# Turning token rows for an expert layer: four TensorE transposes per 128 slots and two copies across partitions

## The chip, the cores and the metric

The kernel runs on one core of one Trainium2 chip. The metric is device time in microseconds for one execution of the whole program. Before the change the median of three runs is 1355.3 us (1355.29 to 1356.96). The profiled execution, from which all other times here are taken, spans 1351.2 us at a granted TensorE clock of 0.995.

## What is computed

Eight sequences of 3584 tokens with 192 channels first pass a causal convolution over 7 tokens, with one softmax-normalised set of taps for each of 8 heads of 24 channels. Then each token goes through one of 8 experts, a two-layer perceptron with 1024 hidden units. The expert is the argmax of the token's own logits, unless a local gate tells the token to keep the expert of the token before it. All numbers are fp32.

```python
x = conv(x, softmax(weight))                       # (8, 3584, 192)
logits = x @ w_gate; local_gate = sigmoid(x @ w_local)
for b in range(B):
    prev_e = -1
    for s in range(S):
        fresh_e = argmax(logits[b, s])
        e = fresh_e if s == 0 or local_gate[b, s] < 0.5 else prev_e   # (or fresh_e if there is none)
        prev_e = e
        p = softmax(logits[b, s])
        h = maximum(x[b, s] @ w1[e], 0.0)          # 192 -> 1024
        out[b, s] = p[e] * (h @ w2[e])             # 1024 -> 192
```

## The kernel before

The 28672 tokens are cut into 16 groups of 1792. For each group the kernel convolves (for most groups ScalarE does the first tap of each head and VectorE the other six), computes the logits, decides the expert of every token, and writes each token's row of 259 words to a place in DRAM that belongs to its expert (`slots`). A row holds the gate factor, the token's number, 192 channels from column `Y0` on, and then 64 channels again, before the token's number once more. The rows go out by indirect DMAs that GpSimd issues (`put`, L777), 128 rows each.

The expert layer reads those rows back in blocks: a single block has 128 slots of one expert (n = 1), a double block has 256 (n = 2). There are 55 singles and 87 doubles in a normal run: singles first, since few rows are ready then, doubles through the middle, and singles at the end for the rests. Two spare blocks at the very end run only if the data need them.

For each block i the order on TensorE is written out by hand:

1. `hidden(i)` (L960): w1 times the turned rows `xT`. The contraction over 192 channels is cut in three steps d of 64. The two 64-row halves of the array work side by side: the upper half makes hidden units 0 to 511 and the lower half 512 to 1023, and each needs all 192 channels, so each holds its own three pieces of 64 channels, with the weights laid out on the host to match. The hidden units come in two lots (`two`), each followed by two relus on ScalarE into `hT` (L965).
2. `turn(i + 1)` (L360 for the transposes, L946 for the copy): the rows `xg` of the next block are turned into `xps` (PSUM), and ScalarE copies them into `xT` (SBUF, one buffer).
3. `output(i)` (L977): w2 times `hT`, for k = 0 and 1 and eight pieces m of the hidden units. The pieces 0, 1, 4, 5 are made by the first pair of relus and come first, the pieces 2, 3, 6, 7 by the second pair. ScalarE (L985) and VectorE (L989) scale and add the two halves' results, and GpSimd scatters them to `out` (L993).

In between, `step(...)` issues convolution and routing work for later groups to ScalarE (L378) and VectorE (L388), and `put(relu)` issues a scatter of rows that waits for the relus. With n = 2 and many rows left to scatter, one more `put` waits for the copy out of `xps` (`copied`). Rows and weights are loaded three blocks ahead, and the load of weights waits until the output matmuls of an earlier block let go of their buffer.

A transpose turns 64 slots (one half of the partitions) by 128 channels. In `turn`, step d takes the 128 channels from 64 d on:

```python
for d in range(KD):                                # 3
    for k in range(n):
        src = xg[:, k, Y0 + d * DR:Y0 + (d + 2) * DR]
        for half in range(2):
            turn_half(at[:, half, d, k, :], src, half)
```

With d = 0 the upper 64 partitions get channels 0 to 63 and the lower ones 64 to 127; with d = 1 they get 64 to 127 and 128 to 191; with d = 2, 128 to 191 and, through the repeated 64 channels of the row, 0 to 63. That makes six transposes per 128 slots, in pairs over the two halves of the slots.

Of the kernel before, what the change touches and what calls it, by code (L numbers as in the profile page):

```python
# [17 lines left out]
P = 128  # L18
B, S, D = 8, 3584, 192
# [11 lines left out]
TB = PT // NB  # L31
# [3 lines left out]
DR = P // 2  # L35
KD = D // DR
FK = F // P
BT = 2 * UT
KT = BT // P
# [22 lines left out]
Y0 = 2  # L62
IX = DG - 1
# [18 lines left out]
def kernel(  # L82
# [10 lines left out]
    nc = tc.nc  # L93
# [44 lines left out]
    with tc.tile_pool(name="scr", bufs=1) as scr:  # L138
        w = scr.tile([1, H, KC], F32, name="w")
# [50 lines left out]
    def z_tile():  # L190
        return yt.tile([P, 3 * NH * TB + NB * DR], F32, name="z")
# [3 lines left out]
    def wide(g, xv, y_sb, both):  # L195

        lps = yps_p.tile([P, 512], F32, name="yps")[:, :4 * TB].rearrange("p (q s) -> p q s", s=TB)  # L200
        count = [0]

        def mine():
            count[0] += 1
            return both and count[0] % 2 == 0

        def convolve(half, heads):
            bs = slice(half * NH, (half + 1) * NH)
            for h in heads:
                ps = hps_p.tile([P, 512], F32, name="hps")[:TB, :NH * GS]  # L210
                nc.tensor.matmul(ps, lhsT=hank[:NI, h, :],
                                 rhs=xv[:NI, bs, h * GS:(h + 1) * GS], start=True, stop=True)
                to = y_sb[:TB, bs, Y0 + h * GS:Y0 + (h + 1) * GS]
                at = ps.rearrange("p (b d) -> p b d", d=GS)
                if mine():
                    nc.vector.tensor_scalar(to, at, rz[:TB, h:h + 1], None, Alu.mult)
                else:
                    nc.scalar.activation(to, at, Act.Copy, scale=rz[:TB, h:h + 1])
                yield

        def again(half):
            bs = slice(half * NH, (half + 1) * NH)
            nc.gpsimd.tensor_copy(yr[:, bs, :], y_sb[:TB, bs, Y0 + P:Y0 + D])
            nc.gpsimd.tensor_copy(y_sb[:TB, bs, Y0 + D:IX], y_sb[:TB, bs, Y0:Y0 + DR])

        def turned(half, qs):
            at = half * 3 * NH // 2
            for q in qs:
                tps = hps_p.tile([P, 512], F32, name="hps")[:, :4 * TB].rearrange(
                    "p (u s) -> p u s", s=TB)  # L230
                for u in range(4):
                    b = half * NH + (q * 4 + u if q < 2 else 2 * u)
                    src = (y_sb[:TB, b, Y0:Y0 + P] if q < 2
                           else yr[:, b:b + 2, :].rearrange("p b d -> p (b d)"))
                    nc.tensor.transpose(tps[:, u, :], src, identity=ident[:TB, :TB])
                leave = nc.vector.tensor_copy if mine() else nc.scalar.copy
                leave(yT[:, at + 4 * q:at + 4 * q + 4, :], tps)
                yield

        def products():  # L240
            for j in range(4):
                u = j // 2 * 3 * NH // 2 + j % 2 * 4
                nc.tensor.matmul(lps[Q * j:Q * j + Q], lhsT=wgb[:, 0, :], rhs=yT[:, u:u + 4, :],
                                 start=True, stop=False, skip_group_check=True)
            for i in range(2):
                for j in range(4):
                    u = j // 2 * 3 * NH // 2 + NH + j % 2 * 2
                    nc.tensor.matmul(lps[Q * j:Q * j + Q, i::2, :], lhsT=wgb[:, 1 + i, :],
                                     rhs=yT[:, u:u + 2, :], start=False, stop=(i == 1),
                                     skip_group_check=True)  # L250

        yield from convolve(0, range(H))
        zy = z_tile()
        yT = zy[:, :3 * NH * TB].rearrange("p (u s) -> p u s", s=TB)
        yr = zy[:TB, 3 * NH * TB:].rearrange("p (b d) -> p b d", d=DR)
        again(0)
        yield from convolve(1, range(5))
        yield from turned(0, (0, 1))
        yield from convolve(1, range(5, H))
        yield from turned(0, (2,))  # L260
        again(1)
        yield from turned(1, range(3))
        products()
        if both:
            nc.vector.tensor_copy(lsb[:, :2, :], lps[:, :2, :])
            nc.scalar.copy(lsb[:, 2:, :], lps[:, 2:, :])
        else:
            nc.scalar.copy(lsb, lps)
        yield
        ltp = yps_p.tile([P, 512], F32, name="yps")[:TB].rearrange("p (q c) -> p q c", c=P)  # L270
        for q in range(4):
            nc.tensor.transpose(ltp[:, q, :], lsb[:, q, :], identity=ident)
        lt = sm.tile([P, NB, E + 1], F32, name="lt")[:TB]
        mark["lt", g] = nc.vector.tensor_copy(lt.rearrange("p (j q) e -> p j q e", q=4),
                              ltp.rearrange("p q (j c) -> p j q c", c=Q)[:, :, :, :E + 1])
        got[g] = lt
# [34 lines left out]
    rows = cst.tile([Q, 2, Q], F32, name="rows")  # L311
# [247 lines left out]
    def gathered(ps):  # L559
        xg = xp.tile([P, KT, DG], F32, name="xg")  # L560
        nc.scalar.copy(xg[:, 0, :Y0 + D], ps[:, :Y0 + D])
        nc.scalar.copy(xg[:, 0, Y0 + D:IX], ps[:, Y0:Y0 + DR])
        nc.scalar.copy(xg.bitcast(I32)[:, 0, IX:], ps[:, 1:2])
        return xg

    def logits(g, y_sb):

        nc.gpsimd.tensor_copy(y_sb[:, :, Y0 + D:IX], y_sb[:, :, Y0:Y0 + DR])  # L568
        z = z_tile()[:, :NT * D].rearrange("p (t d) -> p t d", d=D)
        for t in range(0, NT, TQ):  # L570
            u = min(t + TQ, NT)
            nc.vector.transpose(z[:, t:u, :], y_sb[:, t:u, Y0:Y0 + D])  # L572
            yield 0.2 * (u - t)
        yield "hop"


        lps = [hps_p.tile([P, TQ * Q], F32, name="hps") for half in range(2)]
        begin = [min(TQ * j, NT - TQ) for j in range(4)]
        for b in range(DQ):
            for j in range(4):  # L580
                for half, rows in halves():
                    nc.tensor.matmul(lps[half][Q * j:Q * j + Q, :], lhsT=wgq[rows, b, :],  # L582
                                     rhs=z[rows, begin[j]:begin[j] + TQ, b * Q:(b + 1) * Q],
                                     start=(b == 0), stop=(b == DQ - 1))
        ls = sm.tile([P, 2, TQ * Q], F32, name="ls", bufs=1)
        for half in range(2):
            nc.scalar.copy(ls[:, half, :], lps[half])  # L587
        yield "hop"
        lq = sm.tile([P, 2 * TQ, Q], F32, name="lq", bufs=1)
        nc.vector.transpose(lq.rearrange("p t e -> p (t e)"), ls.rearrange("p h x -> p (h x)"))  # L590
        yield 0.4
        lt = sm.tile([P, NT + 2, E + 1], F32, name="lt")
        for r in range(4):
            for j in range(4):
                t, u = TQ * j, min(TQ * (j + 1), NT)
                at = r // 2 * TQ + t - begin[j]
                e0 = r % 2 * (E + 1)
                nc.vector.tensor_copy(lt[Q * r:Q * r + Q, t:u, :],  # L598
                                      lq[Q * j:Q * j + Q, at:at + u - t, e0:e0 + E + 1])
                yield 0.12  # L600
        return lt
# [328 lines left out]
    def turn(n, xg):  # L930


        xps = xps_p.tile([P, 2, 512], F32, name="xps")
        at = xps[:, :, :KD * BT // 2].rearrange("p h (d k s) -> p h d k s", d=KD, k=KT)
        for d in range(KD):
            for k in range(n):
                src = xg[:, k, Y0 + d * DR:Y0 + (d + 2) * DR]
                for half in range(2):
                    turn_half(at[:, half, d, k, :], src, half)
        xT = tp.tile([P, KD, BT], F32, name="xT")  # L940
        to = xT.rearrange("p d (k h s) -> p h d k s", k=KT, h=2)
        if n == KT:
            to, at = [a.rearrange("p h d k s -> p h (d k) s") for a in (to, at)]
        else:
            to, at = [a[:, :, :, 0, :] for a in (to, at)]
        copied = nc.scalar.copy(to, at)  # L946
        return xT, copied

    def hidden(n, wb, xT, shares=(1, 1)):
# [186 lines left out]
    for i, (_, n, _, _) in enumerate(blocks):  # L1136
# [6 lines left out]
        if i + 1 < len(blocks):  # L1143
            xT, copied = turn(blocks[i + 1][1], xgs[i + 1])
# [6 lines left out]
    kind, _, at, group = spare[0]  # L1151
    any_left = nc.values_load(tabi[kind, group][at:at + 1, 0:1], min_val=0, max_val=DUMMY,  # L1152
                              skip_runtime_bounds_check_because="an entry of the table")
    with tc.If(any_left < DUMMY):
        for block in spare:
# [3 lines left out]
            xg = load_rows(i)  # L1159
# [5 lines left out]
def _w1_layout(np, w1):  # L1165


    w = w1.reshape(E, KD, DR, 2, F // 2).transpose(0, 3, 2, 1, 4)
    w = np.stack([w[:, 0], w[:, 1][:, :, [1, 2, 0]]], 1)
    return w.reshape(E, P, KD * F // 2)  # L1170


# [57 lines left out]
```

## Time and profile before

| what | value |
|---|---|
| time, median of 3 | 1355.3 us |
| hidden matmuls (L960), 6816 | 640.2 us busy |
| output matmuls (L977), 7328 | 652.9 us busy |
| logits matmuls (L582), 1344 | 24.1 us busy |
| evictions on ScalarE (L985), 229 | 86.9 us busy, 379.1 us idle before them |
| ScalarE copy from PSUM, 128 x 64 / 128 x 128 | 218 / 269 ns |
| period of a double block, of a quiet single | 10.80, 5.52 us |
| DMA share, 40 to 268 us / 268 to 1228 / 1228 to 1351 | 0.95 / 0.64 / 0.73 |

In the profile's rows of groups the columns are: line, engine, operation, output and inputs, shapes, count, then busy time in us and mean ns of one, then the idle time just before them and what ended it. The lines of waits give who waited, for whom, the total in us, how often, and the longest. The timeline gives start, length, engine, line, operation and count. fp32 matmuls of L960 and L977 are two instructions each; a transpose is one. PEld is TensorE's load of weights, which lies beside its matmuls.

### The profile page before, as it was taken

What the parts mean: (1) busy time and instruction counts of PE and PEld (TensorE: products, weight loads), DVE (VectorE), ACT (ScalarE), POOL (GpSimd) and SP (SyncE); (2) the same over time, 40 slices, a digit from 0 to 9 for tenths busy, and PEclk for the clock granted to TensorE, in tenths of its full rate; (3) what the DMA queues carried; (4) which work ended last, traced back from release to release, by engine and by line L of the source; (5) the groups of instructions that cost most, each with busy time, mean ns of one, the idle gap of its engine ahead of it and who ended that gap; (6) DMA issues with size and microseconds to landing.
All of it is one profiled execution on the core that took longest, in us unless ns stands there. A gap on an engine that the chain in (4) does not pass through costs nothing. (4 is left out here: it accounts for less than half of the span.)

```text
span 1351.2 us, 41902 instructions
## 1 busy us (share of the span) xinstructions
PE 1327.7 (98%) x17140; PEld 1298.5 (96%) x17140; DVE 780.0 (58%) x2434; ACT 512.1 (38%) x1147; POOL 492.6 (36%) x538
## 2 busy tenths in 40 slices
PE   8899999999999999999999999999999999999998
PEld 7799999999999999999999999999999999999997
DVE  6878887886868787868787878786610000000000
ACT  5244443433343433333334343433333333333333
POOL 4455343534243434343434343434344211221111
PEclk9899999999999999999999999999999999999999
DMA  5899999967575757575757575756566555556993
GB/s 185 291 343 402 365 364 337 389 245 268 199 272 195 289 195 291 198 273 203 280 202 287 196 287 198 289 203 228 199 232 228 199 183 182 190 189 232 322 325 124
DMA packets 67299, 340.39 MB, mean 252 GB/s; under 512 B 12576, under 2 KB 23191, under 8 KB 47650
## 3 DMA queue, kind: packets, MB, share of 16 engines
q1 hardware_dynamic: 44784, 284.88, 58.7%
q0 software_dynamic: 22320, 52.82, 10.3%
q8 instruction: 136, 2.23, 0.6%
q14 instruction: 57, 0.47, 0.1%
q10 hardware_dynamic: 2, 0.00, 0.0%
HBM read 284.73 MB, written 53.41 MB: 250 GB/s over the span
## 5 line engine op out<-in xcount | busy, mean ns | idle before, releaser
L977 PE MATMUL yps<-wb,hT 64*128 64x192 f32 x7328 | 652.9, 326 | 9.6 <-ACT hT L965 7.7
L960 PE MATMUL hps<-xT,wb 64*128 64x256 f32 (+1 forms) x6816 | 640.2, 337 | 0.6 <-issue 0.6
L977 PEld LDWEIGHTS yps<-wb,hT 64*128 64x128 f32 x7328 | 609.7, 188 | 21.0 <-ACT hT L965 14.0
L960 PEld LDWEIGHTS hps<-xT,wb 64*128 64x128 f32 x6816 | 610.0, 188 | 8.4 <-issue 1.8
L993 POOL DMA_INDIRECT out_dram<-o_sb,xg x229 | 232.4, 1015 | 613.7 <-DVE o_sb L989 545.9
L965 ACT ACTIVATE hT<-hps 128x512 f32<-128x512 f32 (+1 forms) x568 | 262.3, 512 | 407.5 <-PE hps L960 306.8
L388 DVE SCALAR_TENSOR_TENSOR y_sb<-x_sb,c,y_sb 128x336 f32<-128x336 f32 x672 | 377.0, 571 | 19.5 <-ACT y_sb L378 1.4
L989 DVE SCALAR_TENSOR_TENSOR o_sb<-yps,xg,o_sb 128x192 f32<-128x192 f32 x229 | 87.4, 413 | 489.1 <-ACT o_sb L985 474.5
L777 POOL DMA_INDIRECT slots<-y_sb,posi x228 | 227.7, 999 | 216.0 <-ACT hT L965 112.0
L985 ACT ACTIVATE o_sb<-yps,xg 128x192 f32<-128x192 f32 x229 | 86.9, 418 | 379.1 <-PE yps L977 368.7
L946 ACT COPY xT<-xps 128x768 f32<-128x768 f32 (+1 forms) x142 | 96.7, 681 | 5.3 <-issue 1.6
L360 PEld LDWEIGHTS xps<-ident,xg 64*128 64x128 f32 x1374 | 81.9, 139 | 2.7
L360 PE MATMUL xps<-ident,xg 64*128 64x64 f32 x1374 | 80.4, 222 | 0.0
L378 ACT ACTIVATE y_sb<-x_sb,c 128x336 f32<-128x336 f32 x112 | 64.6, 589 | 0.0
L572 DVE STREAM_TRANSPOSE z<-y_sb 128x768 f32<-128x768 f32 (+1 forms) x56 | 45.4, 852 | 0.4
L598 DVE COPY lt<-lq 32x36 f32<-32x36 f32 x224 | 41.0, 183 | 3.5
L582 PE MATMUL hps<-z,wg 64*32 64x128 f32 x1344 | 24.1, 272 | 0.7 <-issue 0.6
L582 PEld LDWEIGHTS hps<-z,wg 64*32 64x32 f32 x1344 | 19.1, 105 | 3.4 <-issue 2.6
L556 PE MATMUL yps<-y_sb 112*128 112x194 f32 x64 | 12.5, 351 | 1.8 <-DVE y_sb L550 1.6
L556 PEld LDWEIGHTS yps<-y_sb 112*128 112x128 f32 x64 | 11.2, 201 | 2.6 <-DVE y_sb L550 2.0
L590 DVE STREAM_TRANSPOSE lq<-ls 128x256 f32<-128x256 f32 x14 | 6.2, 444 | 12.4 <-ACT ls L587 12.4
L568 POOL COPY y_sb<-y_sb 128x896 f32<-128x896 f32 x14 | 13.4, 954 | 0.0
(239 smaller groups left out, 374.4 us busy)
## 6 DMA issues: line engine op xcount, KB each, us to landing
wb<-in_w_dram SPq DMA_DIRECT2D x138, 1536.0 KB
x_sb<-in_x_dram SPq DMA_DIRECT2D x14, 1920.0 KB
xg<-slots SPq DMA_DIRECT2D x87, 259.0 KB
xg<-slots SPq DMA_DIRECT2D x53, 129.5 KB
wb<-in_w_dram SPq DMA_DIRECT2D x12, 512.0 KB
out_dram<-o_sb,xg POOLq DMA_INDIRECT x229
slots<-y_sb,posi POOLq DMA_INDIRECT x228
x_sb<-in_xb_dram SPq DMA_DIRECT2D x4, 768.0 KB
```

Of the source, the lines that this page charges most:

```text
L360: nc.tensor.transpose(to, src[rows], identity=ident[rows, rows])
L378: nc.scalar.activation(cols(h), chans(h, 0), Act.Copy, scale=c[:, h, 0:1])
L388: nc.vector.scalar_tensor_tensor(cols(h), chans(h, k), c[:, h, k:k + 1], cols(h), Alu.mult, Alu.add)
L572: nc.vector.transpose(z[:, t:u, :], y_sb[:, t:u, Y0:Y0 + D])
L777: ins = nc.gpsimd.indirect_dma_start(out=slots[:, :], in_=rows, in_offset=None, out_offset=bass.IndirectOffsetOnAxis(ap=to, axis=0)).ins
L946: copied = nc.scalar.copy(to, at)
L960: nc.tensor.matmul(hps[half][:, j, w], lhsT=wb[rows, f0:f0 + P], rhs=xT[rows, d, w], start=(d == 0 and j == 0), stop=(d == KD - 1), skip_g ...
L965: relu = nc.scalar.activation(hT[:, m:m + 2, w], hps[half][:, :, w], Act.Relu)
L977: nc.tensor.matmul(yps[half][:, k * D:(k + 1) * D], lhsT=hT[rows, m, k * P:(k + 1) * P], rhs=wb[rows, WA + m * D:WA + (m + 1) * D], start= ...
L985: nc.scalar.activation(o_sb[:, k, :], y[k][0], Act.Copy, scale=xg[:, k, 0:1])
L989: nc.vector.scalar_tensor_tensor(o_sb[:, k, :], y[k][1], xg[:, k, 0:1], o_sb[:, k, :], Alu.mult, Alu.add)
L993: sent = nc.gpsimd.indirect_dma_start(out=out, in_=o_sb[:, k, :], in_offset=None, out_offset=bass.IndirectOffsetOnAxis(ap=xg.bitcast(I32)[ ...
```

## The change

`turn` makes two steps of 128 channels in place of three overlapping ones. Step 0 puts channels 0 to 63 above and 64 to 127 below; step 1 puts 128 to 191 above and, since the row now repeats channels 128 to 191 and not 0 to 63, the same 128 to 191 below. What is missing is 64 to 127 above and 0 to 63 below. These lie in step 0 on the other half of the partitions, so two further ScalarE copies bring them across, one for each half. One copy out of PSUM becomes three, and six transposes per 128 slots become four. The host lays out w1 for the upper half in the new order of the pieces.

```diff
         def again(half):
             bs = slice(half * NH, (half + 1) * NH)
             nc.gpsimd.tensor_copy(yr[:, bs, :], y_sb[:TB, bs, Y0 + P:Y0 + D])
-            nc.gpsimd.tensor_copy(y_sb[:TB, bs, Y0 + D:IX], y_sb[:TB, bs, Y0:Y0 + DR])
+            nc.gpsimd.tensor_copy(y_sb[:TB, bs, Y0 + D:IX], y_sb[:TB, bs, Y0 + P:Y0 + D])
...
-        nc.scalar.copy(xg[:, 0, Y0 + D:IX], ps[:, Y0:Y0 + DR])
+        nc.scalar.copy(xg[:, 0, Y0 + D:IX], ps[:, Y0 + P:Y0 + D])
...
-        nc.gpsimd.tensor_copy(y_sb[:, :, Y0 + D:IX], y_sb[:, :, Y0:Y0 + DR])
+        nc.gpsimd.tensor_copy(y_sb[:, :, Y0 + D:IX], y_sb[:, :, Y0 + P:Y0 + D])
...
         xps = xps_p.tile([P, 2, 512], F32, name="xps")
-        at = xps[:, :, :KD * BT // 2].rearrange("p h (d k s) -> p h d k s", d=KD, k=KT)
-        for d in range(KD):
+        at = xps[:, :, :BT].rearrange("p h (d k s) -> p h d k s", d=2, k=KT)
+        for d in range(2):
             for k in range(n):
-                src = xg[:, k, Y0 + d * DR:Y0 + (d + 2) * DR]
+                src = xg[:, k, Y0 + d * P:Y0 + (d + 1) * P]
                 for half in range(2):
                     turn_half(at[:, half, d, k, :], src, half)
         xT = tp.tile([P, KD, BT], F32, name="xT")
         to = xT.rearrange("p d (k h s) -> p h d k s", k=KT, h=2)
+        first, by = to[:, :, :2], at
         if n == KT:
-            to, at = [a.rearrange("p h d k s -> p h (d k) s") for a in (to, at)]
+            first, by = [a.rearrange("p h d k s -> p h (d k) s") for a in (first, by)]
         else:
-            to, at = [a[:, :, :, 0, :] for a in (to, at)]
-        copied = nc.scalar.copy(to, at)
+            first, by, to, at = [a[:, :, :, 0, :] for a in (first, by, to, at)]
+        nc.scalar.copy(first, by)
+        for half, rows in halves():
+            copied = nc.scalar.copy(to[rows, :, 2], at[(DR, 0)[half]:(P, DR)[half], :, 0])
         return xT, copied
...
-    w = np.stack([w[:, 0], w[:, 1][:, :, [1, 2, 0]]], 1)
+    w = np.stack([w[:, 0][:, :, [0, 2, 1]], w[:, 1][:, :, [1, 2, 0]]], 1)
```

## The prediction

> **What bounds the kernel now.** I read the busy line first, then the waits of TensorE, then two stretches of the timeline. A block is 128 slots (a single, 55 of them) or 256 (a double, 87): the 142 copies of L946 split so by shape, and 55 + 2 x 87 = 229 slot groups carry the 1374 = 6 x 229 transposes.
>
> ```profile
> PE 1327.7 (98%) x17140; PEld 1298.5 (96%) x17140; DVE 780.0 (58%) x2434; ACT 512.1 (38%) x1147; POOL 492.6 (36%) x538
> ...
> L965 ACT ACTIVATE hT<-hps 128x512 f32<-128x512 f32 (+1 forms) x568 | 262.3, 512 | 407.5 <-PE hps L960 306.8
> ...
> L946 ACT COPY xT<-xps 128x768 f32<-128x768 f32 (+1 forms) x142 | 96.7, 681 | 5.3 <-issue 1.6
> ...
> L360 PE MATMUL xps<-ident,xg 64*128 64x64 f32 x1374 | 80.4, 222 | 0.0
> ```
>
> TensorE is busy 98% of the span and ScalarE 38%. The chain of waits reaches back only 0.7 us, so it says nothing. By the waits of TensorE, all that it loses behind another engine after the start is this, and every one of these waits lies in single blocks (between 268 and 1228 us, the doubles, TensorE waits 1.0 us in all):
>
> ```profile
> PE yps L977 <- ACT hT L965: 7.7, 16, 2.9
> ```
>
> So outside some singles the period of a block is the sum of its TensorE work, and work taken off TensorE shortens the kernel. One undisturbed single, by the timeline (start, length, what):
>
> ```profile
> 1258.98 0.35 PE L360 MATMUL xps<-ident,xg 64*128 64x64 f32 x6
> 1259.10 2.60 PEld L977 LDWEIGHTS yps<-wb,hT 64*128 64x128 f32 x32
> 1259.17 2.83 PE L977 MATMUL yps<-wb,hT 64*128 64x192 f32 x32
> 1259.18 0.66 ACT L965 ACTIVATE hT<-hps 128x256 f32<-128x256 f32 x2 [0.62 <-PE hps L960]
> 1259.72 0.48 ACT L946 COPY xT<-xps 128x384 f32<-128x384 f32 x1
> ...
> 1261.82 0.39 PE L960 MATMUL hps<-xT,wb 64*128 64x128 f32 x4
> ```
>
> Six transposes start at 1258.98 and the output matmuls at 1259.17: 0.19 us, although the row says 0.35. The copy ends at 1260.21, and the hidden matmuls that read it start at 1261.82. A double looks the same: transposes from 1001.41, first output matmul at 1001.78, so 0.37 us for twelve; its copy ends at 1002.86 + 0.81 = 1003.67, and the hidden matmuls start at 1007.03.
>
> A disturbed single, of which there are many between 68 and 268 us:
>
> ```profile
> 180.53 0.97 POOL L777 DMA_INDIRECT slots<-y_sb,posi  x1 [0.30 <-issue]
> 180.58 0.38 PE L977 MATMUL yps<-wb,hT 64*128 64x192 f32 x1
> ...
> 182.04 0.66 ACT L965 ACTIVATE hT<-hps 128x256 f32<-128x256 f32 x2 [2.07 <-PE xps L360]
> 182.48 1.28 PEld L977 LDWEIGHTS yps<-wb,hT 64*128 64x128 f32 x16 [0.53 <-ACT hT L965]
> 182.48 1.57 PE L977 MATMUL yps<-wb,hT 64*128 64x192 f32 x16 [0.23 <-ACT hT L965]
> 182.59 0.48 ACT L946 COPY xT<-xps 128x384 f32<-128x384 f32 x1
> ```
>
> The hidden matmuls are over by 180.71, yet the second pair of relus starts at 182.04, 1.3 us late, 0.54 us after a GpSimd scatter that ran from 180.53 to 181.50. The same holds in the next period (scatter to 187.57, relus at 188.16). Where no scatter runs at that moment the relus start 0.2 us after the transposes do. I take it that TensorE's signals are held up while GpSimd issues a scatter: the trace shows the coincidence, not the mechanism. The second half of the output then waits for the relus, and such a block takes about 6.07 us (copies start at 182.59, 188.70, 194.78) instead of 5.52 (1259.72, 1265.24).
>
> **What the Trainium skill says.** "Perfetto Trace Analysis", Tensor Engine Instruction: the end of a matmul in a profile is computed from its size, not observed. The trace agrees: the rows' 222 ns cannot be what a transpose holds the engine for, since six fit in 0.19 us. "TensorE: Matmul & The Clock Gate", The mechanism (Part 3): matmuls on different row groups run concurrently. The transposes here use the two 64-row halves, and the trace has them in twos, so what is saved is pairs. "ScalarE: Activation LUTs", What ACT_TABLE_LOAD costs: an ACTIVATE with immediates takes 186 ns + 0.833 ns per element, and neighbours overlap by about 93 ns. The copies here agree in slope: 128x384 484 ns and 128x768 806 ns give 0.84 ns per element and 162 ns fixed. No page that I read gives a price for a ScalarE copy from one half of the partitions to the other.
>
> **The change, part by part.**
>
> *Removed: two of six transposes per 128 slots.* That is one pair per single, two per double. Price of a pair: 0.185 / 3 = 61 ns in a single, 0.37 / 6 = 61 ns in a double. The row's busy time would give 80.4 us / 1374 x 2 = 117 ns a pair, but it counts pipeline tails that lie beside the neighbouring matmuls (the TensorE groups of the page sum to over 1400 us in a busy time of 1327.7). The other end is streaming alone: an output matmul of 192 columns takes 5.2 us / 64 = 81 ns, 162 ns a pair, so 64 columns take 54 ns. I take 61.
> - Doubles: 87 x 2 x 61 = 10.6 us, all on the path.
> - Singles that wait for nothing: about 35 x 61 = 2.1 us.
> - Disturbed singles: nothing. TensorE only arrives earlier at a wait that a scatter ends, and that scatter is timed from the end of the block before. I take 20: 16 waits in the TensorE list, and some 20 of the weight loads'.
>
> Sum 12.7 us.
>
> *Changed: one copy becomes three.* By the fit, a single's 384 elements (484 ns) become 256 (377 ns) and two of 128 (270 ns each): 917, so +0.43 us. A double's 768 (806) become 512 (592) and two of 256 (377 each): 1346, so +0.54 us. In all 55 x 0.43 + 87 x 0.54 = 71 us, ScalarE from 512 to 583 us of busy time. None of it is on the path: the room between the end of the copy and the hidden matmuls is 1007.03 - 1003.67 = 3.4 us in a double, 1261.82 - 1260.21 = 1.6 us in a quiet single, and 183.88 - 183.07 = 0.8 us in a disturbed one, each less 0.06 or 0.12 for the pairs removed. Queued behind the copies on ScalarE are the first taps of the convolution (L378, 0.6 us) and the output evictions (L985), which wait for TensorE anyway: ScalarE is idle 369 us before them. In the disturbed single L378 then ends near 184.0 and L985 started at 184.08, so this just fits. GpSimd's scatter put behind the copy (L777, doubles only) waits for the last of the three, but its predecessor on GpSimd runs until 1004.2, about when the third copy ends.
>
> *The unknown price: a copy from partitions 64-127 to 0-63 and back.* No ScalarE row does that. Lower bound: the fit, 0.27 and 0.38 us. Upper bound, my choice: twice the fit; VectorE's small copies between partition groups (L598, 32x36, 183 ns) cost no more than its other small ones. At twice the fit a disturbed single's chain ends at 182.59 + 0.38 + 1.08 = 184.05, 0.17 us late, times 20 = 3.4 us; all others stay hidden. I take the lower, and keep 3.4 us for the range.
>
> *The rest.* The repeated 64 channels come from another column with the same size (L224, L562, L568: same rows, nothing), the weights are reordered on the host, and no other engine's order moves. The last hidden step still needs all three copies, so there is no new wait in front of it but the one counted.
>
> Forecast: 1355.3 - 12.7 = 1342.6 us.
>
> **The rivals.**
> 1. *The early waits go or spread.* The disturbed singles hang on scatters hitting the end of the hidden phase, and a shift by 61 ns can break or set such a sequence. If all 20 went, another 20 x (6.07 - 5.52 + 0.06) = 12 us: 1330. If 15 more joined, 15 x (0.55 + 0.06) = 9 us is lost: 1352. For: both kinds come in runs. Against: the scatter and the hidden phase both count from the end of the previous output, which the change does not touch.
> 2. *The gain is what the busy row says,* 458 x 58.5 ns = 26.8 us: 1328.5. Against: 0.19 us for six.
> 3. *The crossing copies are slow,* 1 us each. Then the chain ends at 1259.72 + 0.38 + 2.0 = 1262.1 in a quiet single, 0.34 us late (x 35 = 12 us), at 184.97 in a disturbed one, 1.1 us late (x 20 = 22 us), still hidden in doubles: 1342.6 + 34 = 1377, slower than before. Against: nothing in the profile shows a copy priced by anything but its elements.
>
> **How the numbers follow.** Forecast, with the upper copy price inside it (1339 to 1347): 0.68. Waits gone, or the full busy time: 0.10. Waits spread: 0.12, ending about 1347 to 1353. Slow copies or a clash that I do not see: 0.10, mostly over 1358. The range 1336 to 1350 takes the forecast's case, half of the spread waits and a part of the vanished ones. Faster by over 0.2% (under 1352.6): 0.68 + 0.10 + most of 0.12 = 0.89; same 0.03; slower 0.08.
>
> **What would show it.** Right: 916 transposes; six in 0.19 us become four in about 0.12, twelve in 0.37 become eight in about 0.25; periods of 10.80 us become 10.68, 5.52 become 5.45, disturbed ones stay at 6.07; L946's successors busy about 168 us in place of 97; no TensorE wait on xT. Wrong: a wait of the hidden matmuls (L960 before) for ScalarE's copies, crossing copies far over 0.4 us, or a list of waits on hT much longer or shorter than 16.

## The result, and the profile after

The changed kernel takes 1339.84 us (1338.32 to 1340.85, four runs) against 1355.3 us for the kernel before on the same chip: ratio 0.9883, 95% interval 0.9866 to 0.99. That is 15.5 us less; the forecast was 12.7 us less.

The page of the changed kernel, first the busy line, then the groups of `turn` (lines have moved down by three: L960, L965, L977, L985, L989, L993 are now L963, L968, L980, L988, L992, L996; the first copy is L947, the two crossing ones are L949):

```profile
PE 1315.2 (98%) x16682; PEld 1264.3 (94%) x16682; DVE 778.6 (58%) x2434; ACT 583.9 (44%) x1431; POOL 492.8 (37%) x538
...
L949 ACT COPY xT<-xps 64x256 f32<-64x256 f32 (+1 forms) x284 | 92.4, 325 | 7.0
L947 ACT COPY xT<-xps 128x512 f32<-128x512 f32 (+1 forms) x142 | 72.2, 509 | 5.9 <-PE xps L360 2.9
...
L360 PE MATMUL xps<-ident,xg 64*128 64x64 f32 x916 | 60.3, 221 | 0.0
```

TensorE is still the bound at 98%, with 458 instructions fewer. ScalarE has risen by 71.8 us, to 44%, and TensorE hardly waits for its copies, as two lines of TensorE's list of waits show (total, times, longest):

```profile
PE yps L980 <- ACT hT L968: 5.3, 16, 0.5
...
PE hps L963 <- ACT xT L947: 0.3, 1, 0.3
```

The first is the old wait of the disturbed singles, again 16 times. The second is the only wait for the copies that this list names.

The timeline of a quiet single of the changed kernel:

```profile
1247.83 0.28 PE L360 MATMUL xps<-ident,xg 64*128 64x64 f32 x4
...
1247.95 2.82 PE L980 MATMUL yps<-wb,hT 64*128 64x192 f32 x32
...
1248.97 0.54 ACT L949 COPY xT<-xps 64x128 f32<-64x128 f32 x2
...
1250.60 2.62 PE L963 MATMUL hps<-xT,wb 64*128 64x128 f32 x44
```

From the first transpose to the first output matmul there are now 0.12 us in place of 0.19. The copies end at 1248.97 + 0.54 = 1249.51, and the hidden matmuls that read them start at 1250.60: 1.09 us of room. A double:

```profile
1196.10 0.41 PE L360 MATMUL xps<-ident,xg 64*128 64x64 f32 x8
...
1196.35 5.42 PE L980 MATMUL yps<-wb,hT 64*128 64x192 f32 x64
...
1197.89 0.76 ACT L949 COPY xT<-xps 64x256 f32<-64x256 f32 x2
...
1201.60 1.67 PE L963 MATMUL hps<-xT,wb 64*128 64x256 f32 x14
```

Eight transposes take 0.25 us in place of 0.37, and 2.95 us of room are left. And a disturbed single:

```profile
187.26 0.28 PE L360 MATMUL xps<-ident,xg 64*128 64x64 f32 x4
187.30 0.97 POOL L777 DMA_INDIRECT slots<-y_sb,posi  x1 [0.30 <-issue]
...
188.79 0.66 ACT L968 ACTIVATE hT<-hps 128x256 f32<-128x256 f32 x2 [1.95 <-PE xps L360]
...
189.74 0.55 ACT L949 COPY xT<-xps 64x128 f32<-64x128 f32 x2
...
190.63 2.84 PE L963 MATMUL hps<-xT,wb 64*128 64x128 f32 x48
```

The relus still start 1.53 us after the transposes, 0.52 us after the scatter's end. Here the copies end at 189.74 + 0.55 = 190.29 and leave 0.34 us before the next hidden matmuls.

Where the time went, from the starts of the blocks in the two traces:

| stretch | before | after | difference |
|---|---|---|---|
| span start to first block | 50.6 us | 53.8 us | +3.1 |
| first block to first double | 216.1 | 213.7 | -2.4 |
| doubles | 961.6 | 950.1 | -11.5 |
| singles at the end | 107.9 | 106.7 | -1.2 |
| end | 15.0 | 15.0 | -0.1 |
| period of a double / of a quiet single | 10.804 / 5.516 | 10.679 / 5.452 | -0.125 / -0.064 |

The late start belongs to that run of the changed kernel: its first load landed 1.1 us later (VectorE starts on it at 3.21 us, before the change at 2.10), TensorE is 1.9 us behind by 13.5 us, and the rest comes at about 45 us. In every other profile here the first block starts between 48.4 and 50.7 us.

### The profile page after: what moved, and what is told of

Its sections match the earlier page's. It is cut to its first block, busy times and chain, and to the rows that moved or that the text cites. A ratio compares the mean times of both kernels' runs of the same rounds, so it can differ in the third digit from the quotient of the medians.

```text
span 1339.1 us, 41274 instructions
## 1 busy us (share of the span) xinstructions
PE 1315.2 (98%) x16682; PEld 1264.3 (94%) x16682; DVE 778.6 (58%) x2434; ACT 583.9 (44%) x1431; POOL 492.8 (37%) x538
## 3 DMA queue, kind: packets, MB, share of 16 engines
q8 instruction: 133, 2.18, 0.6%
## 5 line engine op out<-in xcount | busy, mean ns | idle before, releaser
L980 PE MATMUL yps<-wb,hT 64*128 64x192 f32 x7328 | 647.0, 326 | 8.2 <-ACT hT L968 5.3
L963 PE MATMUL hps<-xT,wb 64*128 64x256 f32 (+1 forms) x6816 | 634.5, 336 | 1.6 <-issue 1.2
L980 PEld LDWEIGHTS yps<-wb,hT 64*128 64x128 f32 x7328 | 603.7, 187 | 19.6 <-ACT hT L968 10.8
L963 PEld LDWEIGHTS hps<-xT,wb 64*128 64x128 f32 x6816 | 585.1, 187 | 28.7 <-issue 3.2
L996 POOL DMA_INDIRECT out_dram<-o_sb,xg x229 | 232.4, 1015 | 608.6 <-DVE o_sb L992 540.1
L968 ACT ACTIVATE hT<-hps 128x512 f32<-128x512 f32 (+1 forms) x568 | 262.1, 512 | 393.1 <-PE hps L963 271.6
L992 DVE SCALAR_TENSOR_TENSOR o_sb<-yps,xg,o_sb 128x192 f32<-128x192 f32 x229 | 87.5, 413 | 475.7 <-ACT o_sb L988 468.5
L988 ACT ACTIVATE o_sb<-yps,xg 128x192 f32<-128x192 f32 x229 | 86.9, 418 | 305.4 <-PE yps L980 299.7
L949 ACT COPY xT<-xps 64x256 f32<-64x256 f32 (+1 forms) x284 | 92.4, 325 | 7.0
L947 ACT COPY xT<-xps 128x512 f32<-128x512 f32 (+1 forms) x142 | 72.2, 509 | 5.9 <-PE xps L360 2.9
L360 PEld LDWEIGHTS xps<-ident,xg 64*128 64x128 f32 x916 | 60.2, 139 | 5.2
L360 PE MATMUL xps<-ident,xg 64*128 64x64 f32 x916 | 60.3, 221 | 0.0
L582 PE MATMUL hps<-z,wg 64*32 64x128 f32 x1344 | 24.1, 272 | 0.7 <-issue 0.5
L582 PEld LDWEIGHTS hps<-z,wg 64*32 64x32 f32 x1344 | 19.0, 105 | 3.1 <-issue 2.3
L556 PE MATMUL yps<-y_sb 112*128 112x194 f32 x64 | 13.8, 377 | 1.8 <-DVE y_sb L550 1.8
```

Source lines behind the costliest of these rows:

```text
L360: nc.tensor.transpose(to, src[rows], identity=ident[rows, rows])
L947: nc.scalar.copy(first, by)
L949: copied = nc.scalar.copy(to[rows, :, 2], at[(DR, 0)[half]:(P, DR)[half], :, 0])
L963: nc.tensor.matmul(hps[half][:, j, w], lhsT=wb[rows, f0:f0 + P], rhs=xT[rows, d, w], start=(d == 0 and j == 0), stop=(d == KD - 1), skip_g ...
L968: relu = nc.scalar.activation(hT[:, m:m + 2, w], hps[half][:, :, w], Act.Relu)
L980: nc.tensor.matmul(yps[half][:, k * D:(k + 1) * D], lhsT=hT[rows, m, k * P:(k + 1) * P], rhs=wb[rows, WA + m * D:WA + (m + 1) * D], start= ...
```

## The experiments

**Theory A:** the gain is the pairs of transposes and nothing else, 61 ns each where TensorE doesn't wait; copies are hidden, crossing costs nothing, and disturbed singles gain nothing. **Rivals:** the gain comes from shifted early waits; the crossing copies eat part of it. **Theory B:** the disturbed singles come from GpSimd's scatters, which hold TensorE's signals up. The kernel before differs by up to 23 us from one comparison to the next. The four groups below ran on four different chips; which chip the first comparison had is not known. So each time is set against the kernel before, or a variant, on the same chip.

### First group: kernel before 1350.6 us

The changed kernel itself did not run on this chip. The kernel with straight copies, the second below, stands for it.

**A third, unread step of transposes put back**, with all three copies kept:

```diff
-        at = xps[:, :, :BT].rearrange("p h (d k s) -> p h d k s", d=2, k=KT)
-        for d in range(2):
+        at = xps[:, :, :KD * BT // 2].rearrange("p h (d k s) -> p h d k s", d=KD, k=KT)
+        for d in range(KD):
...
-                src = xg[:, k, Y0 + d * P:Y0 + (d + 1) * P]
+                src = xg[:, k, Y0 + d % 2 * P:Y0 + (d % 2 + 1) * P]
...
-        first, by = to[:, :, :2], at
+        first, by = to[:, :, :2], at[:, :, :2]
```

> The changed kernel with its three copies, and a third transpose step again (a second turn of channels 128 to 191, whose result nobody reads): six transposes per 128 slots as before, copies as after. Theory A (a pair of transposes costs 61 ns wherever TensorE sets the pace, the copies cost nothing): doubles back at 10.80 us, quiet singles at 5.51, disturbed ones where they are, so 12 to 14 us over the changed kernel, within 2 us of the kernel before. Theory B (a part of the gain comes from the shape of the copies or from the row's new order): the time stays at 1345 or below. Theory C (the three copies do cost, and the pair is worth more than 61 ns): over 1358.

Measured: 1352.11 us, ratio 1.0014 (1.0005 to 1.0023). Double and quiet single are back at 10.806 and 5.516 us. The whole gain is gone with the pairs. By the edit the third step turns channels 0 to 127 again, not 128 to 191 as I wrote; nobody reads the result either way. The interval leaves out 1: with the transposes back at their old number, the two further copies per block, and whatever else differs, cost 0.7 to 3.1 us. Where these lie isn't known, because the kernel before has no profile from this chip.

**The small copies stay on their own partitions** (each half then lacks 64 channels, and holds 64 others twice):

```diff
-            copied = nc.scalar.copy(to[rows, :, 2], at[(DR, 0)[half]:(P, DR)[half], :, 0])
+            copied = nc.scalar.copy(to[rows, :, 2], at[rows, :, 0])
```

> The changed kernel, but the two small copies stay on their own partitions (the third piece of the turned rows is then the wrong 64 channels). Theory A: crossing costs nothing of its own, so the small copies last the same 364 ns (doubles) and 257 ns (singles) and the time is that of the changed kernel, within 0.15%. Rival: the crossing has a price that lies hidden or in the disturbed singles; then these copies are shorter by 20 ns or more, and the time lower by up to 3 us.

Measured: 1338.04 us, ratio 0.9912 (0.99 to 0.9925), 14.1 us under the kernel with the third step. The rows with the shapes kept apart say what crossing costs (busy time and mean ns after the first bar). In the changed kernel, crossing:

```profile
L949 ACT COPY xT<-xps 64x256 f32<-64x256 f32 x174 | 63.8, 367 | 4.3
...
L949 ACT COPY xT<-xps 64x128 f32<-64x128 f32 x110 | 28.6, 260 | 2.7
```

In this kernel, straight:

```profile
L949 ACT COPY xT<-xps 64x256 f32<-64x256 f32 x174 | 64.7, 372 | 2.1
...
L949 ACT COPY xT<-xps 64x128 f32<-64x128 f32 x110 | 29.1, 264 | 1.3
```

A copy from one half of the partitions to the other is no dearer than a straight one. The whole time of the two kernels was not compared on one chip.

**Each crossing copy three times:**

```diff
-            copied = nc.scalar.copy(to[rows, :, 2], at[(DR, 0)[half]:(P, DR)[half], :, 0])
+            for _ in range(3):
+                copied = nc.scalar.copy(to[rows, :, 2], at[(DR, 0)[half]:(P, DR)[half], :, 0])
```

> The changed kernel with each crossing copy made three times: four more ScalarE copies per block. By the changed kernel's trace the last copy ends 0.35 us before the hidden matmuls in a disturbed single (3.01 against 3.36 us after the transposes), 1.1 us in a quiet one (1.69 against 2.77) and 3.0 us in a double (2.54 against 5.50); neighbouring copies follow each other every 0.16 us (singles) and 0.27 us (doubles). Theory A (room as read): quiet singles and doubles keep 5.45 and 10.68 us; disturbed singles end their copies 0.65 us later, so 0.3 us late, and with the tap of the convolution behind them perhaps more: 18 x 0.3 to 0.9 us, 1345 to 1356 in all. Rival (ScalarE's total load counts): 142 x 4 copies of 0.33 us are 185 us more busy time, ScalarE at 57%, and doubles grow as well, so over 1360.

Measured: 1343.71 us, ratio 0.9954 (0.9942 to 0.9966), 5.7 us over the kernel with straight copies and a little under the 1345 to 1356 that I expected. ScalarE is busy 767.2 us, 183 more than in the changed kernel, and the double and the quiet single stand unchanged at 10.679 and 5.452 us. The stretch of early singles grows from 215.6 to 221.2 us, so nearly all of the loss lies there, where the room was smallest (0.34 us in a disturbed single). TensorE's waits (L964 are the hidden matmuls, L950 the copies):

```profile
PE hps L964 <- issue: 4.5, 15, 0.9
...
PE hps L964 <- ACT xT L950: 0.6, 2, 0.3
```

The first line is new in size (1.9 us in the kernel with straight copies); most of what these pauses wait for isn't named by the profile. That doubles and quiet singles don't move fits the room read there, and ScalarE's total load is refuted as a cause. That the early singles lose time because their room is used up is likely, but not traced.

**Both scatters of a single behind its second relus**, so that none of them starts with the first:

```diff
-        hT = hidden(n, wbs[i], xT, (1, 1) if i else (0, 0))
+        hT = hidden(n, wbs[i], xT, ((0, 2) if n == 1 else (1, 1)) if i else (0, 0))
```

> The changed kernel, and in single blocks both scatters of rows wait for the second pair of relus instead of one for each pair; nothing else moves. Theory A (a GpSimd scatter in progress at the end of the hidden phase holds back TensorE's signals, and that makes the 6.04 us singles): no scatter runs there now, most of the 18 to 20 disturbed singles fall to 5.45 us, so 8 to 12 us less, 1328 to 1332. Rival B (those singles are slow for another cause, the load of VectorE or of the DMA queues in that stage): unchanged, 1338 to 1341. Rival C (the scatters land later and the loads of rows wait for them): slower than 1341.

Measured: 1336.66 us, ratio 0.9894 (0.988 to 0.9909). In the two kernels of this chip whose scatters were not moved (straight copies, third step), 17 and 20 second relus start over 1 us after their transposes; here only 3 do. But the time is only 1.4 us under the kernel with straight copies, and the intervals overlap. The timeline shows where the delay went:

```profile
122.19 0.96 POOL L777 DMA_INDIRECT slots<-y_sb,posi  x1 [0.30 <-issue]
122.25 0.98 PE L963 MATMUL hps<-xT,wb 64*128 64x128 f32 x13
...
123.50 1.73 PE L963 MATMUL hps<-xT,wb 64*128 64x128 f32 x26 [0.27 <-issue]
123.67 0.42 ACT L988 ACTIVATE o_sb<-yps,xg 128x192 f32<-128x192 f32 x1 [2.15 <-PE yps L980]
```

The second scatter now falls into the middle of the hidden phase. TensorE stops there and goes on 0.35 us after the scatter's end, and the eviction L988, which normally starts 0.2 us after the hidden matmuls do, starts 1.42 us after them. The delay follows the scatter, as theory B says. My expected time missed, because most of the delay was moved and not removed: eight of the early singles do fall to about 5.45 us, but the two periods with three scatters close together near their logits matmuls (L582), which have pauses now, grow from 8.09 to 11.78 and from 8.00 to 9.51 us against the kernel with straight copies.

### Second group: kernel before 1333.35 us

These runs fell on another chip than the first group, though the first of them was meant as that group's zero.

**The changed kernel, unaltered:**

> The changed kernel itself, unaltered, beside the kernel before on the chip of the other runs, so that the experiments have their own zero. Theory A (2 pairs less per double and 1 less per single, 61 to 62 ns each): ratio to before 0.9900 to 0.9915. If the larger gain of the first comparison holds: 0.987 to 0.989.

Measured: 1319.58 us, ratio 0.9898 (0.9883 to 0.9913), 13.8 us less. No second relu is late, so there are no disturbed singles at all; after the first few blocks the usual period is 5.45 us, with a few longer ones that hold logits matmuls or a wait of another kind. If all 55 singles gain their pair, that is 87 x 0.125 + 55 x 0.064 = 14.4 us, inside the interval of 11.6 to 15.6.

**One step only** (the second step's transposes are left out, its 64 channels are filled from the first):

```diff
-        for d in range(2):
+        for d in range(1):
...
-        nc.scalar.copy(first, by)
+        for d in range(2):
+            nc.scalar.copy(to[:, :, d], at[:, :, 0])
```

> The changed kernel with its second transpose step left out too: two transposes per 128 slots, channels 128 to 191 are replaced by others, and the first copy is made in two. Theory A (each pair is worth the same 61 to 62 ns, however many stand in the row): doubles 10.56 us, quiet singles 5.39, so 12 to 14 us less than the changed kernel. Rival (the last pair hides something, such as the load of the first output weights or the wait for the first relus): the gain is under 8 us.

Measured: 1304.72 us, ratio 0.979 (0.9774 to 0.9806), 14.9 us under the unaltered one, 0.9 us more than I expected. Double 10.553 us, quiet single 5.389: once more 63 ns a pair. The price is linear over both removals. The step from a block's first transpose to its first output matmul says the same (medians of all doubles in the profiles before, after and of this run): 369, 244 and 117 ns for six, four and two pairs.

**Scatters late, and five tiny GpSimd copies behind the first relus**, to see whether GpSimd's work as such delays the signals:

```diff
...
+            if two == 0 and shares == (0, 2) and to_put:
+                for _ in range(5):
+                    spin = nc.gpsimd.tensor_copy(idle, idle)
+                    tc.add_manual_dep(spin.ins, relu.ins.name, SYNC, reason="as the scatter did")
...
-        hT = hidden(n, wbs[i], xT, (1, 1) if i else (0, 0))
+        hT = hidden(n, wbs[i], xT, ((0, 2) if n == 1 else (1, 1)) if i else (0, 0))
```

> Both scatters of a single wait for the second relus, as in the run with late scatters, and where the first scatter used to stand GpSimd now makes five tiny copies on a tile of its own, some 0.9 us that lie over the end of the hidden phase. If any work on GpSimd holds TensorE's signals back, the late relus return (15 or more singles with relus over 1 us late) and the time rises to 1340 or more. If only the issue of a scatter does, it stays as with late scatters: 3 or so late relus, 1335 to 1339.

Measured: 1323.91 us, ratio 0.9932 (0.9919 to 0.9946), two late second relus (1.09 and 2.18 us; in the longer case ScalarE first waits for an output scatter to land). It says nothing on the question: on this chip scatters don't delay the relus either. Its 4.3 us over the unaltered kernel lie mostly in the early singles (204.9 us against 201.4).

**One scatter per single in place of two,** shares (0, 1):

```diff
-        hT = hidden(n, wbs[i], xT, (1, 1) if i else (0, 0))
+        hT = hidden(n, wbs[i], xT, ((0, 1) if n == 1 else (1, 1)) if i else (0, 0))
```

> The changed kernel with one scatter of rows per single, behind the second relus, where a scatter and the hold after it end before the output matmuls do; the rest of the rows goes out when the next loads ask for them. Theory A (a scatter there does no harm): singles fall to 5.45 us, and 1328 to 1334 in all. Rival (rows then come too late and are scattered in bursts before a load that waits for them): slower than 1340.

Measured: 1378.67 us, ratio 1.0341 (1.0327 to 1.0355). The queue that loads the rows waits 108.4 us for scatters, 65.3 us in the unaltered kernel. TensorE waits for rows only twice, 5.7 us in all; mostly it waits for the logits of later groups, which come late seven times, 31 us in all:

```profile
PE hps L582 <- DVE z L572: 31.3, 7, 19.1
```

How the fewer scatters make the logits late isn't traced. On this chip there were no delays to be rid of, so the run shows the price of thinning the scatters out, not what it could save elsewhere.

### Third and fourth group: kernel before 1332.72 and 1354.71 us

**The changed kernel, the late scatters and the tiny copies again, on one chip:**

> The changed kernel, nothing altered, beside the two that follow. In the first comparison 165 signals of hidden matmuls came over 0.2 us late, in the second comparison of the same kernel 2, with the scatters at the same places. Theory H (the delay belongs to the chip and not to the kernel): either over 100 late signals and a ratio to the kernel before near 0.988 (disturbed singles gain nothing), or under 10 and a ratio near 0.9898 (every single gains its pair). Rival (the delay depends on how the first blocks fall in each run): some number in between, 20 to 100.

Measured: 1319.66 us, ratio 0.9903 (0.9888 to 0.9919), no late relu and no late signal. In its timeline a scatter lies on the end of the hidden phase just as in the disturbed single above:

```profile
96.92 0.29 PE L360 MATMUL xps<-ident,xg 64*128 64x64 f32 x4
...
96.95 0.94 POOL L777 DMA_INDIRECT slots<-y_sb,posi  x1 [0.30 <-issue]
...
97.12 0.66 ACT L968 ACTIVATE hT<-hps 128x256 f32<-128x256 f32 x2 [0.62 <-PE hps L963]
```

The scatter starts 0.03 us after the transposes (0.04 above), but the relus start 0.20 us after them, not 1.53.

> The changed kernel with both scatters of a single placed behind the second relus, a second time, now beside the unaltered one on the same chip. If this chip delays signals: late second relus under 5 in place of about 20, but the pause reappears in the middle of the hidden phase where the second scatter now runs, so 0 to 3 us less than e8. If this chip delays none: 0 to 1 us more or less than e8, because the scatters end the chain of their rows a little later and take nothing off TensorE.

Measured: 1320.75 us, ratio 0.9904 (0.9888 to 0.9919): the same as the unaltered kernel. So no version that does the whole work is shown to beat the change.

> The same with five tiny GpSimd copies where the output scatter was (behind the first relus), a second time. If GpSimd's work as such delays TensorE's signals: late second relus come back to about 20, on a chip that delays signals at all. If only a scatter's issue does: at most 3 late relus, and a time 0 to 5 us over e9 (the second comparison had +4.3 us over the unaltered kernel with no late signal, so the copies have a price of their own, by making the scatters behind them later).

Measured: 1324.03 us, ratio 0.9933 (0.9919 to 0.9946), two late second relus (1.15 and 1.67 us): again on a chip without delays, so again no answer.

**The kernel before, in a further comparison:**

> The kernel before, nothing altered, for its profile on the chip that this call gets. Theory H (late signals belong to the chip): on a chip where it takes about 1333 us, the profile shows under 10 late signals of hidden matmuls in place of 211, every single at 5.52 us and the first-block-to-first-double stretch near 201.4 + 50 singles x 0.063 = 204.6 us; on a chip where it takes 1350 to 1356 us, over 100 late signals and about 216 us. Rival (the 22 us between the chips are something else, loads or clock): the count of late signals does not go with the time.

Measured: 1354.8 us, beside 1354.71 for the runs it is compared with (ratio 0.9991 to 1.0009). Its profile has 22 late second relus and 170 late signals, and 215.15 us of early singles. Late signals go with the time:

| kernel before | kernels profiled there | late signals | late second relus | first block to first double |
|---|---|---|---|---|
| 1355.3 us | before, after | 211, 165 | 22, 18 | 216.1, 213.7 us |
| 1350.6 | third step, straight | 199, 192 | 20, 17 | 215.7, 215.6 |
| 1354.7 | before | 170 | 22 | 215.2 |
| 1333.35 | after, one step | 2, 0 | 0, 0 | 201.4, 199.8 |
| 1332.7 | after | 0 | 0 | 200.7 |

A late signal is one of the hidden matmuls that comes over 0.2 us after the end that the trace gives their last instruction; late second relus are counted in singles after the first block. The run with late scatters has 175 late signals, so moving the scatters leaves most of them. In the two profiles of the first line 97 and 77 signals are over 1 us late, and each time a GpSimd scatter (of rows or of outputs) runs between the matmuls' end and the signal. Each chip was met in one group only, so that the chip decides, and not something else about those runs, is inferred. The kernel before has no profile from a chip without delays; that it loses its 20 us there for the same reason is inferred from the changed kernel's traces.

## Why the prediction held, point by point

- **Price of a pair, 61 ns:** right, 2 to 3 ns low. 63 ns from the doubles (0.125 / 2), 64 from the quiet singles, 63 from the next pair taken away.
- **Doubles, 10.6 us:** 87 x 0.125 = 10.9 us by the period; the stretch of doubles shrank by 11.5, but that stretch is a rough measure: 961.6 and 966.1 us in the two profiles of the kernel before.
- **Quiet singles, 2.1 us for 35 of them:** with 22 disturbed before, 33 x 0.064 = 2.1 us. This is a sum, not a reading: only 25 periods of the profile before stand at 5.51 to 5.52 us, the other singles hold further work or waits.
- **Disturbed singles, nothing:** right in the profile, whose disturbed periods are about 6.04 us against 6.07: some 20 x 0.03 = 0.6 us at most. On the two chips without delays there are none, and the gains there fit every single gaining its pair.
- **The term that came out small** is the sum. The measured 15.5 us (13.6 to 18.2 by the interval of the ratio) lie over my 12.7. Part is the price (0.3 us in the doubles). Four disturbed singles fewer in the profile would be 4 x 0.6 = 2.4 us more, but their number in kernels whose transposes and scatters are in the old places (22, 22 and, with the third step, 20) and in those with four (18, 17) is too few to call that an effect of the change. What of the surplus is real stays open: on the chips without delays the gains were 13.8 and 13.1 us, and on another chip with delays the kernel with straight copies gained 12.6 us (10.1 to 13.5). That this nearly equals the forecast is in part luck: counted from the kernel with the third step the pairs gave 14.1 us there, and 0.7 to 3.1 us went the other way.
- **Copies hidden:** right in the blocks that were read. Rooms of 1.09, 2.95 and 0.34 us against 1.1, 2.7 and 0.4 from the prediction's numbers. Over the whole kernel the third-step run leaves a cost of 0.7 to 3.1 us. Busy time of the copies 164.6 us for 168.
- **Crossing copies at the price of straight ones:** right, 260 and 367 ns for the fit's 270 and 377. By the Trainium skill, "ScalarE: Activation LUTs", What ACT_TABLE_LOAD costs, an estimate for an ACTIVATE of these sizes is 186 + 0.833 x 128 = 293 and 399 ns; for these copies the measurement decides, and it is some 32 ns lower.
- **What would show it:** 916 transposes, 0.12 and 0.25 us, periods of 10.68 and 5.45 us, and 16 waits on hT all came. One TensorE wait on xT, of 0.3 us, was not foreseen.
- **Rivals:** the busy row's 117 ns a pair is refuted by the periods (63 ns), slow crossing copies by the straight ones. The early waits neither went nor spread: 22 late second relus before, 18 after.
- **What I took for the cause of the disturbed singles** was half of it. That the delay follows a scatter is borne out by the late scatters. That a scatter alone suffices is not: the same scatter at the same moment delays nothing on two of the chips. What differs between the chips, and whether other work of GpSimd would delay signals as well, is not settled; both tries at the latter fell on chips without delays.

## What to carry to other kernels

Price instructions of a full engine by the step in time to the next group of instructions that does other work, not by their busy rows; here the row gave 117 ns and the step 61, and the step held over two removals in a row. Moving work to an engine that is half idle cost little here (at most 3.1 us), because there was room between its end and its first reader. Read that room in each kind of block, the tightest one above all. Before a delay is put down to the program, see whether it is there on another chip.

## What the runs showed of the hardware that I had not expected

- The same program differs by 1.5% between two chips at the same granted clock (0.994 to 0.998): 1339.84 and 1319.66 us. Of the 21 us between their profiled spans (1339.1 and 1317.7) 13 lie in the early singles, where TensorE's signals beside a scatter often come 1.3 us late on the one chip and at once on the other.
- A ScalarE copy between the two halves of the partitions costs what a straight one does: 260 and 264 ns for 64 x 128, 367 and 372 for 64 x 256.
- Tripling ScalarE's small copies (183 us more of busy time) cost 5.7 us, nearly all of it in the early singles, where the rooms that were read are 0.3 to 1.1 us.
